# One more pair of MLP chunks in seven products, twelve operand splits on GpSimd, and holds in the order model

## The chip, the core and the metric

The kernel runs on one core of a Trainium2 chip. The core has five engines that run side by side and wait for each other by semaphores: TensorE (PE in the profile; PEld is its weight load), VectorE (DVE), ScalarE (ACT), GpSimd (POOL) and SyncE (SP), which here only issues transfers. On-chip data lies in SBUF, 128 partitions wide; TensorE writes to PSUM, eight banks of 128 x 512 float32. Inputs and outputs lie in DRAM. The metric is the time of one execution on the device, in microseconds; a kernel's time is the median of several runs.

## The reference

Everything is float32. `x` has 2048 tokens of 512 features. Two branches read the layer-normed tokens, and the result is the sum of both and of `x`:

```python
xn = _layernorm(x)                                    # over the 512 features
q, k, v = split(xn @ wqkv)                            # 32 heads of 16
pq, pk = phi(q), phi(k)                               # phi(t) = (t + 1 if t > 0 else exp(t)) + 1e-6
kv, z  = einsum("bhsd,bhse->bhde", pk, v), pk.sum over tokens
o      = einsum(pq, kv) / (einsum(pq, z) + 1e-6)      # linear attention
h      = relu(xn @ w1 + b1) ** 2                      # 1376 hidden columns
return x + o @ wo + (h @ w2 + b2)
```

## The kernel before

**Float32 from two parts.** TensorE multiplies in a format with fewer bits. So every operand is split in two: ScalarE copies it into the short format (the high part), and a second engine subtracts that from the original (the low part). A product then takes three passes: high with high, high with low, low with high. `split(h, l, src, eh, el)` does the two steps, `el` naming the engine of the subtraction; `ops_of` (line 522) splits a weight operand and stores it to DRAM for later use; `parts_of` (line 948) splits an activation.

**Stages.** The 2048 tokens are 16 tiles of 128, or four blocks of 512.
1. The start, to about 105 us: for each tile the layer norm (`bn_stats`, `bn_aggr`, then the small `y` operations of `normalise`, which make the root of the variance, and the tile `xp`), the tile turned (on TensorE for the first eight, by moves `xg` on the sync queue and VectorE transposes for the rest), the projection on k (`ps <- wk, xs`), phi, and the sum `acc <- pk, tok` that becomes kv. GpSimd makes the low part of `tok` here.
2. A round `n = 0` for token blocks 3 and 2, to about 257 us, and a round `n = 1` for blocks 1 and 0. Each goes over seven pairs of 128 columns, `k = 0` to 6: two pairs of q (`NQ = 2`) and five of the hidden columns of the MLP (`NP = 5`); a last, narrower chunk `z` is apart.

**Seven products instead of eight.** Two blocks of tokens against two halves of the features and two chunks of columns is a 2x2 by 2x2 product. The first layer (`"1"`) makes it with seven products, with sums of weight quarters as operands (`make_1`, i = 0, 1: plain, 2 to 5: sums, 6: plain). The second layer (`"2"`), from the pair's four results `h[k, 0..3]` to the output, has two forms. In the plain one each of the four results is split and multiplied with both halves of its w2 rows, eight calls of `second` (line 923), six 128x512 matmuls each (two chunks of 128 output columns, three passes). In the seven-product one VectorE first makes four sums of the results (`combinations`, line 1356), seven activations are split, and seven calls follow, one of each of seven kinds, with w2 operands of plain quarters (`make_m`, `make_m3`) and of sums of quarters (`make_t`). In round 1 all pairs use seven. In round 0 only the two q pairs do (their "w2 rows" are a matrix that the kernel made of kv and wo); the five MLP pairs are plain: their first two results right in the loop (`add_product`), the last two behind the seven products (`plain`). The operands of sums for round 1 (`t` for the MLP pairs) are made in a spare moment at the end of round 0 and the begin of round 1, from rows read a second time (`raw_t`, `made`).

**Buffers.** Weight operands pass through eight SBUF buffers `D0` to `D7` in the order of a list, `needed_in`; in round 0 an entry makes the operand and stores it, otherwise it loads it back. `fetch_raws` reads raw weights into up to four buffers in the order of `raw_jobs`.

**The order of the work.** All operations are recorded first (so every row of the profile has the line of the recorder, 301). `Program.order` then plays the program 150 times with a cost model: TensorE keeps the recorded order, and each other engine takes, of its tasks that are ready, the one with the earliest due time (line 277). After each play the due times of what TensorE waited for are pressed earlier, and the best play's order is emitted. In the model a task with `lock` (lines 155 and 158) waits for the one before it with `lock`: the two-input operations of VectorE with both inputs in SBUF, if they have more than 64 elements, and GpSimd's subtractions.

Of the kernel before, what the change touches and what calls it, by code (L numbers as in the profile page):

```python
# [15 lines left out]
LAST = 3  # L16
REORDER = True
# [57 lines left out]
class Program:  # L75
# [163 lines left out]
    def play(self):  # L239
# [18 lines left out]
        while done < len(ts):  # L258
# [54 lines left out]
def kernel(  # L313
# [20 lines left out]
    TB = 4  # L334
# [110 lines left out]
    NK = NQ + NP  # L445
    wd1 = [dram.tile([4, P, 2, 512], F32, name=f"wd1_{k}") for k in range(NK)]
# [160 lines left out]
    def make_m3(o):  # L607
        for e, k in enumerate((NP, NP + 1)):
            parts_in(o[:, e:e + 1], raw_of[f"2_{k}"][0][:, 1:, 256:])
            spill("2", k, 3, o[:, e:e + 1])  # L610
        m_done(NP, NP + 1)

    def make_t(k, e):

        def make(o):
            raw = f"{'t' if k < NP else '2'}_{k}"
# [9 lines left out]
            if k >= NP:  # L626
                m_done(k)
            elif e:
                raw_done(raw)
# [206 lines left out]
    def needed_in(n):  # L836
# [6 lines left out]
        for p in range(NK + 1):  # L843
# [5 lines left out]
            if f >= 0 and n == 0:  # L849
                both_of("2", f, 0, make_2(f, 0))  # L850
# [6 lines left out]
            if p < NK:  # L857
                both_of("1", p, 4, make_1(p, 4) if direct else None)
                if f >= 0 and n == 0:
# [4 lines left out]
        if n == 0:  # L864
            for k in (NP, NP + 1):
                o.append(([("2", k, 0), ("2", k, 2)], make_m(k)))
                if k == NP:
                    both_of("2", NP - 1, 2, make_2(NP - 1, 1))
            for k in (NP, NP + 1):
                for e in range(2):  # L870
                    both_of("2", k, 4 + 2 * e, make_t(k, e))
            both_of("z", 0, 2, make_z(1))
            o.append(([("2", NP, 3), ("2", NP + 1, 3)], make_m3))
            for f in range(NP):
# [283 lines left out]
    for k in range(NP):  # L1158
        if k + 1 < NP:
            raw_jobs.append(raw_1(NQ + k + 1))  # L1160
        raw_jobs.append(raw_2(k))
    raw_jobs += [raw_2(NP), raw_2(NP + 1), RAW_Z[1]]
# [137 lines left out]
    for n in range(2):  # L1300
# [5 lines left out]
        def slots_of(k):  # L1306
# [8 lines left out]
            else:  # L1315
                t = four(f"rf{k}", f"r{(1, 4, 5)[(k - NQ) // 2]}")
                for e in range(2):
                    slots[k + e] = [None, None, t[:, 2 * e], t[:, 2 * e + 1]]
            return slots[k]
# [4 lines left out]
        def finish(k, i, src):  # L1324
# [9 lines left out]
            else:  # L1334
# [5 lines left out]
                if i < 2:  # L1340
# [15 lines left out]
        def combinations(k):  # L1356

            a, b, c, d = (h[k, i] for i in range(4))
            o = s2[k // 4][:, k % 4] if n else w512(f"s2_{k}", "p", 6)
# [16 lines left out]
        for p in range(NK + 1):  # L1376
# [20 lines left out]
            if f_before:  # L1397
# [4 lines left out]
                add_product(p - 1, 0)  # L1402
# [20 lines left out]
            if f_before:  # L1423
# [36 lines left out]
        if n == 0:  # L1460
            jobs = []
            b = [bank(f"late{k}", loop_tag) for k in range(TB)]
            X, V, Z, Y = b[1:3], [b[3], b[0]], acc[:2], acc[2:]

            def product_job(ps, k, i, first=False, last=False):

                def source():
                    if i not in (0, 2) and k not in h:
                        run(*combinations(k))
                    return h[k, i // 2] if i in (0, 2) else h[k][i]  # L1470

                jobs.append((source, lambda s: second(ps, ("2", NP + k, i), s, first, last)))

            for k in range(NQ):
                product_job(X, k, 0, k == 0)
# [4 lines left out]
            for k in range(NQ):  # L1480
                product_job(V, k, 4, k == 0)
            at_end(lambda: o.update(m5=copies("m5", V)))
            for k in range(NQ):
                product_job(X, k, 5)
# [3 lines left out]
            for k in range(NQ):  # L1488
                product_job(X, k, 6)
            at_end(lambda: o.update(u3=copies("u3", X)))  # L1490
            for k in range(NQ):
                product_job(Y, k, 3, False, k == NQ - 1)
            at_end(lambda: (add_to(o["m5"], Y), turned_to(t1, 2, o["m5"]), store(res[t1], t1, 1)))
            for k in range(NQ):
                product_job(X, k, 7)
# [14 lines left out]
            for k in range(NQ, NK):  # L1510
# [11 lines left out]
            def step(e):  # L1522
# [3 lines left out]
                if e > 3:  # L1526
                    if not made_t and sorted(raw_free) == ["rp0", "rp1", "x0", "x1"]:
# [3 lines left out]
                    if len(raw_free) < 4:  # L1531
                        for u in range(2 * (len(made_t) < NP)):
# [4 lines left out]
            assert len(made_t) >= NP, made_t  # L1537
# [86 lines left out]
```

## Time and profile before

| | |
|---|---|
| median of 3 runs | 409.05 us (408.73 to 409.63) |
| the profiled execution's own time | 408.82 us |
| its span in the profile | 407.1 us |
| TensorE busy | 399.6 us, 1793 matmuls |
| VectorE busy | 353.2 us, 600 instructions |
| ScalarE busy | 269.4 us |
| GpSimd busy | 28.0 us |
| transfers | 95.68 MB, mean 235 GB/s |

A row of a group names engine, operation, what is written and read, shape and count, then busy time and mean of one in ns, then the idle time before these instructions and what ended it. A row of a timeline has the start and the length in us, and in brackets the idle time ahead. Names have no buffer numbers: `ops` are weight operands, `s` split activations, `c` and `rf` the results of MLP pairs in round 0, `rr` other results, `ps` and `acc` the PSUM banks. A busy TensorE is not TensorE at its peak, since its matmuls overlap.

### The profile page before, as it was taken

The numbers are of one execution on the slowest core, as the hardware profiler recorded it, in microseconds if no ns is written. First come the engines' busy times: TensorE is split into PE (matmuls) and PEld (weight loads), VectorE is DVE, ScalarE is ACT, GpSimd is POOL, SyncE is SP. The second block draws the span as 40 slices with busy tenths as digits, with TensorE's granted clock in tenths as the row PEclk, the third lists the DMA queues.
The fourth block names the chain that finished last, engine by engine and source line by source line (L and its number), as shares of the span: only waits on it lengthen the run. The fifth ranks groups of instructions, "written<-read, shape, count | busy, mean of one in ns | idle before, by whom it ended". The sixth has DMA issues, their size and how long they took to land.

```text
span 407.1 us, 5594 instructions
## 1 busy us (share of the span) xinstructions
PE 399.6 (98%) x1793; PEld 330.4 (81%) x1793; DVE 353.2 (87%) x600; ACT 269.4 (66%) x461; POOL 28.0 (7%) x50
## 2 busy tenths in 40 slices
PE   8999999999999999999999999999999999999994
PEld 7787888788888888888888888888888888888883
DVE  5899898799878898999889989899989989786784
ACT  5785665675858897889886343366888777545440
POOL 2232322220000000000000000000000000000001
PEclk9999999999999999999999999999999999999999
DMA  7871455933997679667359998999767789979424
GB/s 230 292 194 43 104 155 125 280 100 151 327 323 287 233 280 306 248 241 260 155 194 361 258 339 275 370 298 330 280 223 271 263 219 258 256 277 281 157 54 103
DMA packets 78674, 95.68 MB, mean 235 GB/s; under 512 B 39186, under 2 KB 50450, under 8 KB 78388
## 3 DMA queue, kind: packets, MB, share of 16 engines
q1 hardware_dynamic: 76404, 94.53, 73.4%
q10 hardware_dynamic: 2144, 0.52, 0.6%
q0 software_dynamic: 96, 0.26, 0.3%
q8 instruction: 14, 0.23, 0.2%
q14 instruction: 16, 0.13, 0.1%
HBM read 57.81 MB, written 35.39 MB: 229 GB/s over the span
## 4 chain that ended last, share of the span: by engine, by line
PE 95%; DVE 2%; DMA 1%; ACT 1%; issue 0%
PE ps L301 52%; PE acc L301 42%; DMA x<-in_A_x_dram 1%; DVE y L301 1%; DVE xp L301 0%; DVE res L301 0%; DVE o L301 0%; DVE st L301 0%; ACT k L301 0%; DVE pk L301 0%; DVE xs0l L301 0%; ACT t L301 0%; ACT xs0h L301 0%; DVE mv L301 0%
## 5 line engine op out<-in xcount | busy, mean ns | idle before, releaser
L301 PE MATMUL ps<-s,ops 128*128 128x512 f32 x405 | 94.9, 389 | 0.0
L301 PEld LDWEIGHTS ps<-s,ops 128*128 128x128 f32 x405 | 76.0, 188 | 15.8
L301 PE MATMUL acc<-s,ops 128*128 128x512 f32 (+1 forms) x270 | 62.2, 382 | 0.0
L301 PEld LDWEIGHTS acc<-s,ops 128*128 128x128 f32 x270 | 49.6, 188 | 9.9
L301 ACT ACTIVATE s<-rr 128x512 fp32r<-128x512 f32 x54 | 33.8, 631 | 20.9 <-DVE s L301 12.0
L301 PE MATMUL acc<-pk,tok 128*128 128x512 f32 x192 | 47.2, 394 | 0.0
L301 DVE TENSOR_TENSOR s<-rr,s 128x512 fp32r<-128x512 f32 x54 | 36.8, 688 | 11.8 <-ACT s L301 10.6
L301 PEld LDWEIGHTS acc<-pk,tok 128*128 128x128 f32 x192 | 35.4, 188 | 8.3 <-DVE pk L301 0.6
L301 PE MATMUL ps<-T,ops 128*128 128x512 f32 x168 | 41.4, 390 | 0.0
L301 PE MATMUL acc<-T,ops 128*128 128x512 f32 x168 | 41.2, 389 | 0.0
L301 PEld LDWEIGHTS acc<-T,ops 128*128 128x128 f32 x168 | 31.5, 188 | 6.6
L301 PEld LDWEIGHTS ps<-T,ops 128*128 128x128 f32 x168 | 31.5, 188 | 6.5
L301 POOL TENSOR_TENSOR tok<-xp,tok 128x512 fp32r<-128x512 f32 x16 | 21.5, 1347 | 43.8 <-ACT tok L301 43.8
L301 PE MATMUL ps<-xs0h,ops 128*128 128x512 f32 x72 | 23.7, 389 | 0.0
L301 ACT ACTIVATE rr<-acc 128x512 f32<-128x512 f32 x23 | 13.6, 589 | 11.5 <-PE acc L301 11.1
L301 DVE TENSOR_TENSOR ops<-raw,ops 128x512 fp32r<-128x512 f32 (+1 forms) x28 | 18.7, 676 | 1.6 <-ACT ops L301 1.6
L301 ACT ACTIVATE ops<-raw 128x512 fp32r<-128x512 f32 (+1 forms) x28 | 15.8, 576 | 5.2 <-PE acc L301 1.8
L301 PE MATMUL acc<-xs0h,ops 128*128 128x512 f32 x56 | 18.4, 389 | 0.0
L301 DVE TENSOR_TENSOR rr<-acc,rr 128x512 f32<-128x512 f32 x21 | 14.4, 687 | 2.9 <-PE acc L301 1.6
L301 POOL DMA_DIRECT2D out_dram<-res x2 | 1.5, 729 | 215.5 <-DVE res L301 213.0
L301 ACT ACTIVATE k<-ps 128x512 f32<-128x512 f32 x16 | 9.5, 593 | 10.1 <-PE ps L301 9.9
L301 PEld LDWEIGHTS ps<-xs0h,ops 128*128 128x128 f32 x72 | 13.5, 188 | 2.8
(158 smaller groups left out, 772.1 us busy)
## 6 DMA issues: line engine op xcount, KB each, us to landing
wd<-ops SPq DMA_DIRECT2D x35, 512.0 KB, 4.8
ops<-wd SPq DMA_DIRECT2D x31, 512.0 KB, 5.5
ops<-wd SPq DMA_DIRECT2D x56, 256.0 KB, 4.1
wd<-made SPq DMA_DIRECT2D x10, 512.0 KB, 5.9
res<-in_A_x_dram SPq DMA_DIRECT2D x32, 128.0 KB, 5.6
wd<-ops SPq DMA_DIRECT2D x13, 256.0 KB, 3.7
out_dram<-res SPq DMA_DIRECT2D x24, 128.0 KB, 4.7
x<-in_A_x_dram SPq DMA_DIRECT2D x5, 512.0 KB, 5.9
```

The source lines that it names most:

```text
L301: getattr(getattr(self.nc, t.engine), t.name)(*map(real, t.args), **{k: real(a) for k, a in t.kw.items()})
```

## The change

Three parts. (1) `SEVEN = 1`: in round 0 the last MLP pair (k = 6, w2 rows 4) joins the two q pairs in the seven products. Its four results are squared at once and kept; the call of `second` for it in the loop and its two plain jobs are gone; the place of the former is taken by the first two products of the first q pair. Its operands for w2 are made by `make_m`, `make_t`, `make_m3` from one buffer of raw rows, and the `t` operands of this pair are stored then, not made later; its rows are fetched last. Each pair's sums are now made in two steps, with the products of kind 4 and of kind 5. (2) In `make_1` the low part of operands i = 2 and 4, for k = 1 to 6, goes to GpSimd: twelve splits, two of them for a q pair, each of a tile with two operands. (3) In the order model the condition on the size is dropped, and where the chosen task has a lock that is held, one that can start is taken before it.

```diff
+SEVEN = 1
...
-            t.lock = t.name in ("tensor_tensor", "scalar_tensor_tensor") and n > 64 and not any(map(in_psum, ins))
+            t.lock = t.name in ("tensor_tensor", "scalar_tensor_tensor") and not any(map(in_psum, ins))
...
                 t = min((t for t in waiting[e] if t.ready <= when + 0.1), key=lambda t: (t.due, t.index))
+                if t.lock and locked > when + 0.1:
+                    t = min((t for t in waiting[e] if max(t.ready, locked * t.lock) <= when + 0.1), key=lambda t: (t.due, t.index), default=t)
...
+    late_pairs = tuple(range(NK - SEVEN, NK))
+    seven_rows = (*range(NP, NP + NQ), *range(NP - SEVEN, NP))
...
-            ops_of(o, "1", k, i, src)
+            ops_of(o, "1", k, i, src, "pool" if k and i in (2, 4) else "dve")
...
-            for k in (NP, NP + 1):
+            for k in seven_rows:
                 o.append(([("2", k, 0), ("2", k, 2)], make_m(k)))
-                if k == NP:
-                    both_of("2", NP - 1, 2, make_2(NP - 1, 1))
-            for k in (NP, NP + 1):
+            for k in seven_rows:
                 for e in range(2):
                     both_of("2", k, 4 + 2 * e, make_t(k, e))
...
-            for f in range(NP):
+            for f in range(NP - SEVEN):
                 for i in (0, 2):
                     both_of("2", f, i)
...
-    raw_jobs += [raw_2(NP), raw_2(NP + 1), RAW_Z[1]]
+    raw_jobs += [raw_2(NP), raw_2(NP + 1), RAW_Z[1], *map(raw_2, seven_rows[NQ:])]
...
-                add_product(p - 1, 0)
+                if n or p - 1 not in late_pairs:
+                    add_product(p - 1, 0)
+                else:
+                    b = [bank(f"late{k}", loop_tag) for k in range(TB)]
+                    X, V, Z, Y = b[1:3], [b[3], b[0]], acc[:2], acc[2:]
+                    for i, ps in ((0, X), (2, Z)):
+                        second(ps, ("2", NP, i), parts_of("s", h[0, i // 2]), i == 0)
...
+            pairs = (*range(NQ), *late_pairs)
+            todo = {}
...
+            def phase(ps, i, first=False, last=False):
+                for k in pairs:
+                    product_job(ps, k, i, first and k == 0, last and k == pairs[-1])
+
+            for k in pairs[1:]:
+                product_job(X, k, 0)
                 product_job(Z, k, 2)
-                if k == 0:
-                    jobs.append((None, lambda s: add_product(NK - 1, 1)))
...
-            for k in range(NQ):
-                product_job(V, k, 4, k == 0)
+            phase(V, 4, True)
...
-            for k in range(NQ, NK):
+            for k in range(NQ, NK - SEVEN):
                 for i in range(2):
                     plain(k, i)
...
-                        raw_jobs.extend(raw_2(k, "t") for k in range(NP))
+                        raw_jobs.extend(raw_2(k, "t") for k in range(NP - SEVEN))
```

More of the change, by code (lines that the diff above doesn't have):

```diff
@@ L605, in make_m, with make_m3 @@
         return make
-    def make_m3(o):
-        for e, k in enumerate((NP, NP + 1)):
+    def make_m3(o, *ks):
+        for e, k in enumerate(ks):
             parts_in(o[:, e:e + 1], raw_of[f"2_{k}"][0][:, 1:, 256:])
             spill("2", k, 3, o[:, e:e + 1])
-        m_done(NP, NP + 1)
+        m_done(*ks)
     def make_t(k, e):
         def make(o):
-            raw = f"{'t' if k < NP else '2'}_{k}"
+            raw = f"{'2' if k in seven_rows else 't'}_{k}"
             (b11, b12), (b21, b22) = ((t[:, 0], t[:, 1]) for t in (by_halves(raw_of[raw][0][:, e]) for e in range(2)))
@@ L625, in make @@
             ops_of(o, "2", k, 4 + 2 * e, by_chunks(src))
-            if k >= NP:
+            if k in seven_rows:
                 m_done(k)
@@ L848, in needed_in @@
                 both_of("1", p, 2, make_1(p, 2) if direct else None)
-            if f >= 0 and n == 0:
+            if f >= 0 and n == 0 and f not in seven_rows:
                 both_of("2", f, 0, make_2(f, 0))
@@ L858, in needed_in @@
                 both_of("1", p, 4, make_1(p, 4) if direct else None)
-                if f >= 0 and n == 0:
+                if f >= 0 and n == 0 and f not in seven_rows:
                     both_of("2", f, 2, make_2(f, 1))
@@ L1339, in finish @@
                 h[k, i] = o
-                if i < 2:
+                if n == 0 and k in late_pairs:
+                    square(o)
+                elif i < 2:
                     square(o)
@@ L1422 @@
             finish(p, 2, R[2])
-            if f_before:
+            if f_before and (n or p - 1 not in late_pairs):
                 add_product(p - 1, 1)
@@ L1461 @@
             jobs = []
-            b = [bank(f"late{k}", loop_tag) for k in range(TB)]
-            X, V, Z, Y = b[1:3], [b[3], b[0]], acc[:2], acc[2:]
+            pairs = (*range(NQ), *late_pairs)
+            todo = {}
             def product_job(ps, k, i, first=False, last=False):
                 def source():
[L1468 to L1472, printed above, removed]
-            for k in range(NQ):
-                product_job(X, k, 0, k == 0)
+                    if i in (0, 2):
+                        return h[k, i // 2]
+                    if i == 4:
+                        todo[k] = combinations(k)
+                    if i in (4, 5):
+                        todo[k].pop(0)()
+                    return h[k][i]
+                jobs.append((source, lambda s: second(ps, ("2", row_of(k), i), s, first, last)))
+            def phase(ps, i, first=False, last=False):
[3 more added lines that the diff above has]
+                product_job(X, k, 0)
                 product_job(Z, k, 2)
-                if k == 0:
-                    jobs.append((None, lambda s: add_product(NK - 1, 1)))
             at_end(lambda: o.update(m1=copies("m1", X)))
-            for k in range(NQ):
-                product_job(V, k, 4, k == 0)
+            phase(V, 4, True)
             at_end(lambda: o.update(m5=copies("m5", V)))
-            for k in range(NQ):
-                product_job(X, k, 5)
+            phase(X, 5)
             at_end(lambda: add_to(o["m5"], X))
@@ L1526, in step @@
                 if e > 3:
[L1527 removed]
+                    if not made_t and not raw_of and not raw_jobs:
+                        assert sorted(raw_free) == ["rp0", "rp1", "x0", "x1"]
                         raw_free[:] = ["x0", "x1"]
[L1529 removed]
+                        raw_jobs.extend(raw_2(k, "t") for k in range(NP - SEVEN))
                         fetch_raws()
[L1531 to L1532 removed]
+                    if made_t or "t_0" in raw_of:
+                        for u in range(2 * (len(made_t) < NP - SEVEN)):
                             make_t(len(made_t), u)(work.tile([P, 2, 512], F32R, name="made", tag=f"rp{u}"))
```

25 lines of the change are left out of this document (14 added, 11 removed).

## The prediction

> **What bounds the kernel now.** I read the page first (engines, clock, chain), then the chain of waits in order of time, then the timeline of each engine where the chain leaves TensorE, then groups of lines by window.
>
> ```profile
> span 407.1 us, 5594 instructions
> PE 399.6 (98%) x1793; PEld 330.4 (81%) x1793; DVE 353.2 (87%) x600; ACT 269.4 (66%) x461; POOL 28.0 (7%) x50
> PEclk9999999999999999999999999999999999999999
> PE 95%; DVE 2%; DMA 1%; ACT 1%; issue 0%
> ```
> ```profile
> 0.81 2.71 DMA x<-in_A_x_dram
> ...
> 75.20 2.72 PE ps L301 x12
> 77.93 3.01 PE acc L301 x12
> 80.94 2.72 PE ps L301 x12
> ...
> 128.09 14.96 PE ps L301 x66
> ...
> 224.65 32.64 PE ps L301 x144
> ...
> 390.61 8.85 PE ps L301 x39
> ```
>
> The page gives TensorE 95% of the chain at a full clock all along. The chain shows how full it is: 32.64 / 144 and 14.96 / 66 are both 0.227 us for a 128x512 matmul, the same as 2.72 / 12. So from 81 us to the last matmul TensorE runs without a gap, VectorE's 87% notwithstanding, and there a matmul less is worth 0.227 us. Only ahead of 81 us do I find lost time: 3.01 where twelve matmuls take 2.72 (0.29 us), and two more places:
>
> ```profile
> 31.07 1.07 PE L301 MATMUL ps<-wkh,xs0l 128*128 128x512 f32 x4
> 32.59 0.65 PE L301 MATMUL ps<-ident,xp 128*128 128x128 f32 x4 [0.46 <-DVE xp L301]
> ...
> 37.66 1.07 PE L301 MATMUL ps<-wkh,xs0l 128*128 128x512 f32 x4
> 38.65 0.66 PE L301 MATMUL ps<-ident,xp 128*128 128x128 f32 x4
> ```
>
> Four matmuls from 31.07 occupy 0.91 us, so the transposes could start at 31.98 and start at 32.59: 0.61 us lost. In the same way 37.66 + 0.91 = 38.57 against 38.65: 0.08. What is late at 32.59 is the normalised tile xp, and VectorE and GpSimd tell why:
>
> ```profile
> 30.32 1.25 DVE L301 SCALAR_TENSOR_TENSOR y<-mv,y 128x2 f32<-128x2 f32 x1
> 31.60 0.36 DVE L301 SCALAR_TENSOR_TENSOR y<-y 128x2 f32<-128x2 f32 x2
> 31.99 1.92 DVE L301 TENSOR_SCALAR xp<-x,mv,y 128x512 f32<-128x512 f32 x4
> ...
> 30.02 1.53 POOL L301 TENSOR_TENSOR tok<-xp,tok 128x512 fp32r<-128x512 f32 x1 [3.21 <-ACT tok L301]
> ...
> 25.55 0.63 ACT L301 ACTIVATE ops<-raw_z 128x512 fp32r<-128x512 f32 x1 [1.07 <-DMA raw_z<-in_B_w_dram]
> 26.25 0.60 ACT L301 ACTIVATE k<-ps 128x512 f32<-128x512 f32 x1
> ```
>
> A two-element operation on y takes 1.25 us, where two of its kind take 0.36 together: it stands behind GpSimd's split of tok (30.02 to 31.55). Before that, ScalarE stood 1.07 us for the load of raw_z, with k behind it. At 75 us VectorE stands for another load, and the 0.29 follows:
>
> ```profile
> 75.23 0.69 DVE L301 TENSOR_TENSOR wv<-wv,raw_v 128x512 f32<-128x512 f32 x1 [2.40 <-DMA raw_v<-in_A_wqkv_dram]
> ```
>
> **The change, part by part.**
>
> *The pair in seven products.* In the first round a plain pair costs eight calls of `second`, the seven-product form seven; a call is six matmuls. Order of the built programs: TensorE issues six 128x512 matmuls fewer, nothing else on it is added. They leave the gapless stretch: 6 x 0.227 = **-1.36 us**. The pair's last two chunks no longer feed TensorE directly behind their relu; their place there is taken by the first attention pair, long finished, so no wait is added.
>
> What it puts on the others lies mostly at 204 to 257 us, where the seven products and the plain pairs run; the first row is of that window, the other two are of the spare operands made for round 1, of the window 245 to 320 us:
>
> ```profile
> 204.00:257.00 53.00, 53.00 (x236) 43.88 (x235) 48.46 (x73) 25.62 (x42) 0.00 (x0) 1.00 0.93 289
> ...
> L301 DVE TENSOR_TENSOR made<-t,made 128x512 fp32r<-128x512 f32 x10 | 6.8, 683 | 0.0
> L301 DVE TENSOR_TENSOR t<-raw_t,t 128x256 f32<-128x256 f32 x10 | 4.2, 422 | 0.2
> ```
>
> VectorE gains three splits and four sums, seven times about 0.69 us: +4.8. The pair's transposed sums and their splits (four operations of 0.42, two of 0.68, 3.0 us) move in from behind 257 us. 48.5 + 7.8 = 56.3 us against the 51.6 that TensorE then takes: by busy time VectorE would be the new bound. But the records of neighbours overlap:
>
> ```profile
> 163.91 0.69 DVE L301 SCALAR_TENSOR_TENSOR rr<-rr,dr 128x512 f32<-128x512 f32 x1
> 164.52 0.69 DVE L301 TENSOR_TENSOR s<-c,s 128x512 fp32r<-128x512 f32 x1
> 165.12 0.68 DVE L301 TENSOR_TENSOR rf<-ps,rf 128x512 f32<-128x512 f32 x1
> 165.72 0.68 DVE L301 TENSOR_TENSOR ops<-s,ops 128x512 fp32r<-128x512 f32 x1
> ```
>
> They start 0.60 us apart and are recorded as 0.69, so the real need is nearer 56.3 x 0.60 / 0.69 = 49.0 us of 51.6, and part of the work there (the split x and the sums for round 1) may also wait until TensorE is in round 1. I take 0 for this part; the other end is that VectorE lags by one operation, 0.7 us, at three of the phases, +2.1. ScalarE gains three copies of 0.63 in a stretch where it is busy 25.6 of 53: 0, by that row.
>
> The pair's w2 rows now stay in their raw buffer until all of the pair's operands are made. In the issue order of the sync queue five transfers of 512 KB are gone (a second load of the raw rows, two stores of spare operands, two reloads) and three stores of 256 KB are added: 1.8 MB less, in a stretch whose transfers are busy at 0.93. The only transfer in the chain is the first load of x, at 0.81 us; I take 0, with a late operand load at +0.5 on the far side.
>
> *GpSimd's twelve splits.* These are what moves, who runs them, and what it costs VectorE when it meets one:
>
> ```profile
> L301 DVE TENSOR_TENSOR ops<-s,ops 128x512 fp32r<-128x512 f32 x12 | 8.2, 680 | 0.0
> L301 DVE TENSOR_TENSOR s<-c,s 128x512 fp32r<-128x512 f32 x9 | 6.1, 674 | 1.0 <-ACT s L301 1.0
> ...
> 65.45 1.78 DVE L301 TENSOR_TENSOR ops<-raw,ops 128x512 fp32r<-128x512 f32 x1
> 67.16 0.68 DVE L301 TENSOR_TENSOR ops<-raw_z,ops 128x512 fp32r<-128x512 f32 x1
> ...
> 65.35 1.34 POOL L301 TENSOR_TENSOR tok<-xp,tok 128x512 fp32r<-128x512 f32 x1 [3.09 <-ACT tok L301]
> ```
>
> The first two rows are of the window 97 to 197 us. VectorE loses 8.2 us; GpSimd, idle there, gains 12 x 1.34 = 16 us. The operand is ready 0.65 us later for the product and for its store to DRAM; the eight buffers ahead of TensorE hide that. A VectorE operation with both inputs in SBUF that is issued under GpSimd's split takes 1.78 instead of 0.68: up to 1.10 lost per split, 13.2 us for twelve, more than the 8.2 saved. The Trainium skill (SBUF — State Buffer, Who interferes with whom) says so too: a VectorE instruction with two SBUF inputs and a GpSimd instruction that reads SBUF exclude each other for the whole instruction. By that rule the edit alone is a loss for VectorE of up to 5.0 us of its time; the trace agrees (1.78 against 0.68). Were all of it on TensorE's path, the sum would be 5.0 higher, 411.7. What counts for the time is whether a held operation is one that TensorE awaits:
>
> ```profile
> 163.51 0.63 ACT L301 ACTIVATE s<-c 128x512 fp32r<-128x512 f32 x1
> 164.05 0.58 ACT L301 ACTIVATE rf<-ps 128x512 f32<-128x512 f32 x1
> 164.53 0.62 ACT L301 ACTIVATE ops<-s 128x512 fp32r<-128x512 f32 x1
> ...
> 164.64 1.75 PE L301 MATMUL acc<-s,ops 128*128 128x512 f32 x7
> ```
>
> This is the tightest place of a step. The split s<-c ends on VectorE at 165.21; TensorE reads it with its fifth matmul, at 164.64 + 4 x 0.227 = 165.55: 0.34 us to spare. A hold of 1.10 in front of it costs 0.76. In the new order ScalarE's copy for GpSimd stands behind its copy for s<-c in these steps, so GpSimd can begin some 0.5 us after VectorE may (the ScalarE rows start 0.54 and 0.48 apart), and behind s<-c come an operation from PSUM, a reciprocal and a transpose, with one SBUF input each. I take 0, far end 9 x 0.76 = +6.8, near end 0: VectorE freed of 8.2 us cannot speed a gapless TensorE.
>
> *The order model.* It now counts a hold for operations of any size, and passes over a held task for a free one. It changes the order of VectorE, ScalarE and the sync queue from about 23 us on; TensorE's order and the order behind the last matmul stay. The second y group (the one of 30.32) now stands directly behind pk and one bn_stats instead of behind two bn_stats, k, xs0l and pk, and ahead of the tok split; its roots on ScalarE, still behind raw_z, stand behind xs0h alone instead of behind k, k, xs0h, t and pk. That is some four VectorE operations of 0.6 us and the hold earlier, against a lateness of 0.61: I count **-0.61**, and **-0.08** for the next tile, whose y is likewise earlier. The subtraction from wv that waited 2.40 us now stands behind k and pk of the next tile, and the load of raw_v ahead of a store on the sync queue: **-0.29**. Each can come back elsewhere among so many short dependences; far end of the three together 0, or +0.5 when the new order has a wait of its own.
>
> *Sum.* The profiled execution took 408.82 us. 408.82 - 1.36 - 0.61 - 0.08 - 0.29 = 406.48. It lies 0.23 under the median of 409.05, so the forecast for the median is **406.7 us**. The end is untouched: from 399.46 on the old order stands.
>
> **The rivals.**
>
> *Only the six matmuls count.* The start's waits are only moved. For it: so many small dependences, and the loads of raw_z and raw_v land when they land. Against it: the y group is earlier by more than its lateness. 409.05 - 1.36 = 407.7.
>
> *VectorE becomes the bound between 204 and 257 us.* For it: 56.3 of 51.6 by busy time, 49.0 by starts. Against it: what can wait there. Three lags of 0.7 give back 2.1 of what was won: 406.7 + 2.1 = 408.8, no measurable change.
>
> *GpSimd's hold falls on the awaited splits.* Slower: each held s<-c costs 0.76; from four of the nine on (3.0 us) the gain of 2.3 is gone. Five give 406.7 + 3.8 = 410.5, all nine 413.5. For it: the rows at 65.45 show the hold in full; GpSimd starts when its input is there, not when the order model thinks. Against it: the order of ScalarE's copies.
>
> **How the numbers follow.** The forecast (all of the sum) has 0.55, only the six matmuls 0.22, VectorE as the bound 0.13, the hold 0.10. A measurement of this kernel tells about 0.2%, 0.8 us, from no change. Faster by more: the first two and a little of the third, 0.79; within: 0.12; slower: 0.09. The range 406.2 to 408.6 reaches from 0.5 under the forecast (the first 30 us may give some more) over 407.7 to the edge of the third case. The forecast alone would be 406.3 to 407.2.
>
> **What would show it.** Right: 1787 matmuls; from 81 us on groups of 0.227 us a matmul; no 0.46 before ident,xp at 32 us; twelve rows ops<-s on GpSimd near 1.3 us; VectorE nearly full from 204 to 257 us, and TensorE without a gap there. Wrong: TensorE behind DVE s or POOL ops in the list of waits; a y row of over 1 us again ahead of an xp that TensorE awaits; a piece of the chain between 110 and 200 us above 0.227 us a matmul.

## The result, and the profile after

The changed kernel takes 406.94 us (median of six runs, 406.76 to 407.24), the kernel before took 409.35 us beside it (median of six, 408.73 to 410.06). The ratio is 0.9941, with a 95% interval of 0.9929 to 0.9954: 2.4 us faster, where 406.7 was forecast. The execution that was profiled took 407.24 us, the longest of its six, over a span of 405.5 us; that of before had 408.82. So the two profiled executions are only 1.58 us apart; the rest of the 2.4 lies between executions.

The page of the changed kernel, its first rows and the shares of its chain:

```profile
span 405.5 us, 5588 instructions
PE 397.9 (98%) x1787; PEld 329.3 (81%) x1787; DVE 353.6 (87%) x595; ACT 270.7 (67%) x464; POOL 46.3 (11%) x62
DMA packets 78258, 93.85 MB, mean 231 GB/s; under 512 B 39154, under 2 KB 50418, under 8 KB 77972
PE 96%; DVE 2%; DMA 1%; issue 0%
```

The six matmuls are gone (1793 to 1787), and so are the 1.8 MB. GpSimd has its twelve splits, 18.3 us more busy than before, but VectorE is as busy as it was (353.2 before), although it has five instructions fewer. TensorE still makes the chain, and in its two longest pieces on `ps` it runs at the same pace as before:

```profile
127.02 14.96 PE ps L304 x66
...
163.74 2.88 PE acc L304 x12
...
226.64 28.56 PE ps L304 x126
```

28.56 / 126 = 0.227 us a matmul, also where the third pair of seven products runs. But two short pieces stand out: twelve matmuls from 163.74 take 2.88, not 2.72 us, and twelve from 178.85 take 2.91. The start, in the timelines of VectorE, GpSimd and TensorE:

```profile
27.78 0.16 DVE L304 SCALAR_TENSOR_TENSOR y<-mv,y 128x2 f32<-128x2 f32 x1 [0.52 <-ACT y L304]
27.98 0.36 DVE L304 SCALAR_TENSOR_TENSOR y<-y 128x2 f32<-128x2 f32 x2
28.37 0.55 DVE L304 TENSOR_SCALAR xp<-x,mv,y 128x512 f32<-128x512 f32 x1
...
30.75 1.30 POOL L304 TENSOR_TENSOR tok<-xp,tok 128x512 fp32r<-128x512 f32 x1 [3.89 <-DVE st L304]
...
31.10 1.07 PE L304 MATMUL ps<-wkh,xs0l 128*128 128x512 f32 x4
32.01 0.60 PE L304 MATMUL ps<-ident,xp 128*128 128x128 f32 x4
```

The y operation that lasted 1.25 us now lasts 0.16 and ends 2.8 us before GpSimd's split of tok begins, and the transposes follow the matmuls ahead of them without a gap (31.10 + 0.91 = 32.01).

For all kernels below I use one account, worked out from the starts of the matmuls in the trace, from the 41st (at 10.2 to 10.7 us) to the last: every distance over 0.26 us counts as a wait with what it has above 0.227, and the rest of the stretch is TensorE without waits. Before: 390.76 us, of which 1.80 are waits. After: 388.70, of which 1.17 are waits. Without waits that is 388.96 and 387.52, or 1.44 less; the waits give 0.63. Short ones that every kernel has, 0.09 to 0.11 each and most of them where TensorE turns to another accumulator, are 0.86 us of each sum, which is all that the kernel with the fewest has left (e12). The account is of one profiled execution each, and it ends at the last matmul. Behind that the changed kernel lost some of its lead: from VectorE's last operation to the end of the span, with the last stores under way, 4.5 us passed before (402.57 to 407.1) and 5.0 after (400.53 to 405.5). Over all fourteen profiled executions the time from the start of the last matmul to the end of the span lies between 5.6 and 6.6 us; why it varies isn't known.

### The profile page after: what moved, and what is told of

Same layout as the page of the kernel before. It is cut to its first block, busy times and chain, and to the rows that moved or that the text cites. A ratio compares the mean times of both kernels' runs of the same rounds, so it can differ in the third digit from the quotient of the medians.

```text
span 405.5 us, 5588 instructions
## 1 busy us (share of the span) xinstructions
PE 397.9 (98%) x1787; PEld 329.3 (81%) x1787; DVE 353.6 (87%) x595; ACT 270.7 (67%) x464; POOL 46.3 (11%) x62
## 4 chain that ended last, share of the span: by engine, by line
PE 96%; DVE 2%; DMA 1%; issue 0%
PE ps L304 53%; PE acc L304 43%; DMA x<-in_A_x_dram 1%; DVE res L304 0%; DVE o L304 0%; DVE st L304 0%; DVE xp L304 0%; DVE y L304 0%; DVE mv L304 0%
## 5 line engine op out<-in xcount | busy, mean ns | idle before, releaser
L304 PE MATMUL ps<-s,ops 128*128 128x512 f32 x411 | 96.4, 389 | 0.0
L304 PEld LDWEIGHTS ps<-s,ops 128*128 128x128 f32 x411 | 77.1, 188 | 16.0
L304 PE MATMUL acc<-s,ops 128*128 128x512 f32 (+1 forms) x258 | 59.8, 383 | 0.0
L304 PEld LDWEIGHTS acc<-s,ops 128*128 128x128 f32 x258 | 47.2, 188 | 9.9 <-ACT s L304 0.5
L304 ACT ACTIVATE s<-rr 128x512 fp32r<-128x512 f32 x56 | 34.9, 630 | 21.1 <-DVE s L304 11.0
L304 DVE TENSOR_TENSOR s<-rr,s 128x512 fp32r<-128x512 f32 x56 | 38.1, 686 | 9.4 <-ACT s L304 8.3
L304 POOL TENSOR_TENSOR tok<-xp,tok 128x512 fp32r<-128x512 f32 x16 | 23.1, 1442 | 43.7 <-ACT tok L304 26.9
L304 POOL TENSOR_TENSOR ops<-s,ops 128x512 fp32r<-128x512 f32 x12 | 16.7, 1396 | 75.5 <-ACT ops L304 58.1
L304 DVE TENSOR_TENSOR ops<-raw,ops 128x512 fp32r<-128x512 f32 (+1 forms) x28 | 17.4, 630 | 0.7 <-ACT ops L304 0.5
```

The lines of the kernel that those rows point to most:

```text
L304: getattr(getattr(self.nc, t.engine), t.name)(*map(real, t.args), **{k: real(a) for k, a in t.kw.items()})
```

## The experiments

My theory was the sum of the prediction: six matmuls, plus start's waits that the two lines of the order model remove, with the GpSimd splits worth nothing. The rivals: that any edit makes the planner draw another order, and the waits come and go with it; that the splits are needed, since VectorE has more to do with a third pair in seven products; that their holds cost time.

| kernel | pair k = 6 | splits | model | median, us | ratio to before | waits | without waits |
|---|---|---|---|---|---|---|---|
| before | eight | VectorE | old | 408.9 to 409.4 | 1 | 1.80 | 388.96 |
| e1 | eight | VectorE | new | 408.42 | 0.9984 (0.9975 to 0.9993) | 1.67 | 388.84 |
| e3 | eight | GpSimd | old | 408.33 | 0.9984 (0.9975 to 0.9993) | 1.52 | 388.78 |
| e6 | eight | GpSimd, order of before | old | 408.84 | 0.9996 (0.9987 to 1.0005) | 2.07 | 388.89 |
| e8 | eight | VectorE, redrawn | old | 408.36 | 0.9985 (0.9976 to 0.9994) | 1.45 | 388.84 |
| e9 | eight | VectorE, order of before, repaired | old | 407.99 | 0.9969 (0.9956 to 0.9981) | 1.33 | 388.79 |
| e2 | seven | VectorE | old | 408.44 | 0.9993 (0.9984 to 1.0002) | 1.92 | 387.63 |
| e4 | seven | VectorE | new | 409.01 | 0.9999 (0.9990 to 1.0008) | 3.12 | 387.47 |
| e11 | seven | GpSimd | old | 408.07 | 0.9970 (0.9960 to 0.9980) | 3.16 | 387.49 |
| after | seven | GpSimd | new | 406.94 | 0.9941 (0.9929 to 0.9954) | 1.17 | 387.52 |
| e5 | seven | VectorE, order of after | new | 407.12 | 0.9952 (0.9940 to 0.9965) | 1.25 | 387.55 |
| e7 | seven | GpSimd, redrawn | new | 406.37 | 0.9936 (0.9924 to 0.9949) | 1.08 | 387.51 |
| e10 | seven | GpSimd, order of after, two swaps | new | 406.70 | 0.9934 (0.9921 to 0.9946) | 0.98 | 387.37 |
| e12 | seven | GpSimd, redrawn again | new | 406.60 | 0.9933 (0.9921 to 0.9946) | 0.86 | 387.37 |

### One part alone, and all but the splits

The order model alone, on the kernel before:

```diff
-            t.lock = ... and n > 64 and not any(map(in_psum, ins))
+            t.lock = ... and not any(map(in_psum, ins))
...
+                if t.lock and locked > when + 0.1:
+                    t = min((t for t in waiting[e] if max(t.ready, locked * t.lock) <= when + 0.1), ...)
```

> The kernel before with the two lines of the order model alone: 1793 matmuls, no split on GpSimd added, eight calls for the pair k = 6. My theory (the lines of the model remove the start's waits): the waits of 0.61 us ahead of ident,xp at 32.6 us, 0.08 at 38.7 and 0.29 at 78 us go and nothing takes their place: 0.98 us less, a ratio of 0.9976. Rival (re-planning): any edit makes the planner draw another order, and the start's waits come and go by chance: then this kernel has waits of its own before 81 us, of a sum that may lie on either side of 0.98 us, ratio 0.999 to 1.001. Rival (six matmuls only): ratio 1.000.

0.9984, 0.6 us. The waits at 32.6 and 78 us are gone, but a longer one stands at 26.49, and it is of the very kind that the new lines describe. Its rows, in the timelines of VectorE, GpSimd and TensorE:

```profile
24.90 0.57 DVE L303 SCALAR_TENSOR_TENSOR y<-mv,y 128x3 f32<-128x3 f32 x1
25.89 0.55 DVE L303 TENSOR_SCALAR xp<-x,mv,y 128x512 f32<-128x512 f32 x1
...
24.15 1.29 POOL L303 TENSOR_TENSOR tok<-xp,tok 128x512 fp32r<-128x512 f32 x1 [0.89 <-ACT tok L303]
...
26.49 0.66 PE L303 MATMUL ps<-ident,xp 128*128 128x128 f32 x4 [0.66 <-DVE xp L303]
```

The tile xp is late by 0.82 us, and only part of that is the hold of y (0.57 instead of 0.16): the group simply stands late in this order.

The seven products alone (the diff of the change without the lines above and without the splits):

> The kernel before with the seven products for the pair k = 6 alone: no GpSimd splits, old model. My theory: six matmuls of 0.227 us less, 1.36 us, a ratio of 0.9967, with the start's waits of 0.98 us still there. Rival (VectorE becomes the bound between 204 and 257 us): three or more lags of 0.7 us of TensorE behind VectorE there, 2.1 us back, a ratio near 1.002. Rival (re-planning): the start's waits differ from those of before although the model is the same, and the ratio lies off 0.9967 by that difference.

0.9993, most of the six matmuls' gain lost. Without waits TensorE needs 387.63, as the changed kernel, but the waits are not where either theory put them. The start has none at 32 or 78 us, although the model is the old one, and from 204 to 257 us there are only 0.2 us of them. The largest stands at 150, here with VectorE's row ahead of it:

```profile
148.54 0.69 DVE L302 TENSOR_TENSOR rf<-ps,rf 128x512 f32<-128x512 f32 x1
149.15 0.68 DVE L302 TENSOR_TENSOR s<-c,s 128x512 fp32r<-128x512 f32 x1
...
149.88 0.72 PE L302 MATMUL acc<-s,ops 128*128 128x512 f32 x2 [0.39 <-DVE s L302]
```

Its s<-c stands behind a transpose and rf<-ps, where before had it ahead of rf (164.52 in the prediction's rows): 0.56 us of TensorE for a place in a queue, as these rows read.

The splits alone:

```diff
-            ops_of(o, "1", k, i, src)
+            ops_of(o, "1", k, i, src, "pool" if k and i in (2, 4) else "dve")
```

> The kernel before with the twelve splits on GpSimd alone: old model, eight calls for the pair k = 6. My theory: VectorE is freed of 8 us and TensorE does not move: ratio 1.000, start's waits as before. Rival (the hold): the old order does not know where GpSimd stands, and each s<-c split that falls under a GpSimd split costs TensorE 0.76 us: for four of nine 3.0 us, a ratio of 1.007. Rival (copies): ScalarE's copies for GpSimd stand ahead of its copies for s<-c and cost TensorE 0.1 to 0.23 us each, a few tenths in all.

0.9984. No loss by holds, and again a start without its waits, with the old model; small ones stand at 220 us instead.

The changed kernel with the splits back on VectorE:

```diff
-            ops_of(o, "1", k, i, src, "pool" if k and i in (2, 4) else "dve")
+            ops_of(o, "1", k, i, src)
```

> The changed kernel with the twelve splits back on VectorE: seven products for k = 6 and the new model stay. My theory (the splits are worth nothing to TensorE): as the changed kernel, a ratio of 0.994; the three small waits of TensorE behind ScalarE's copies at 163.9, 179.0 and 277.1 us, 0.1 us each at the matmul, may go, for 0.996 to 0.993. Rival (relief): with seven products VectorE needs the 8 us that GpSimd takes off it; without them TensorE waits for VectorE's s or c rows, 0.7 us or more in all, a ratio of 0.996 or above.

0.9999: the whole gain is gone. That looks like the relief. But of its 3.12 us of waits, 0.88 stand at 32.8 us, ahead of ident,xp, where none of the twelve splits is concerned. VectorE and GpSimd show what is late there:

```profile
29.55 1.96 DVE L304 TENSOR_SCALAR xp<-x,mv,y 128x512 f32<-128x512 f32 x2
...
32.20 0.55 DVE L304 TENSOR_SCALAR xp<-x,mv,y 128x512 f32<-128x512 f32 x1
...
29.76 1.46 POOL L304 TENSOR_TENSOR tok<-xp,tok 128x512 fp32r<-128x512 f32 x1 [2.99 <-ACT tok L304]
```

Two xp in a row take 1.96 us here and 1.00 us in the changed kernel (at 33.31): the second begins under GpSimd's split of tok. This is a hold of 0.96 us, on an operation with one input of 512 elements, and neither order model has it, since both lock two-input operations alone. VectorE has no gap from there to the xp at 32.20 that TensorE awaits, so by these rows this hold is the whole wait; no run here removes it to test that.

The largest of the other waits is one for a single copy of ScalarE, which itself waited for VectorE's t. Timelines of ScalarE and TensorE:

```profile
210.96 0.67 ACT L304 ACTIVATE ops<-t 128x512 fp32r<-128x512 f32 x1 [1.03 <-DVE t L304]
...
211.69 1.22 PE L304 MATMUL ps<-s,ops 128*128 128x512 f32 x3 [0.42 <-ACT ops L304]
```

Four kernels, four different sets of waits. So a part can't be priced by building it in or out: the planner draws the whole order anew each time.

### The splits with the order held still

In the next two the plan is made as in the changed kernel (or as before), and only when the tasks are emitted is the engine of the twelve subtractions exchanged. Every queue keeps its order; nothing else differs.

```diff
-            getattr(getattr(self.nc, t.engine), t.name)(
+            getattr(getattr(self.nc, "vector" if t.moved else t.engine), t.name)(
...
         split(o[:, 0], o[:, 1], src, "act", el)
+        nc.tasks[-1].moved = el == "pool"
```

> The changed kernel with its planned order kept in every queue, only the twelve subtractions carried out by VectorE at the places of that order instead of GpSimd. Theory (relief: with the pair in seven products VectorE needs the twelve operations taken off it): twelve times 0.60 us come back on VectorE where s<-c had 0.36 to 0.45 us to spare, so TensorE waits behind VectorE's s or c rows between 97 and 257 us, 1.3 us in all as in the two kernels with seven products and without the splits (gaps of 1.26 and 1.39 us there), a time of 408.2 or more. Rival (the planner's draw: the lags of those two kernels are of their own orders): no gap, 406.9, a ratio of 0.994 to before.

407.12 us against 406.94 (ratios 0.9952 and 0.9941, with intervals that overlap), and the waits are 1.25 against 1.17: the runs can't tell the two apart, with or without GpSimd. In this order the relief is not needed. The page of this kernel, a window of it, and the same window with the one behind it in the changed kernel (length, then busy time of PE, PEld, DVE, ACT and POOL, clock, share of the DMA engines, GB/s):

```profile
PE 397.8 (98%) x1787; PEld 329.1 (81%) x1787; DVE 356.1 (88%) x607; ACT 270.5 (67%) x464; POOL 29.5 (7%) x50
```

```profile
97.00:197.00 100.00, 100.00 (x457) 82.80 (x456) 90.74 (x159) 83.61 (x139) 0.52 (x1) 1.00 0.77 268
```

```profile
97.00:197.00 100.00, 100.00 (x457) 82.94 (x456) 88.42 (x147) 83.72 (x139) 17.27 (x13) 1.00 0.77 267
204.00:257.00 53.00, 53.00 (x235) 43.88 (x235) 48.82 (x73) 25.35 (x43) 0.00 (x0) 1.00 0.93 272
```

Twelve operations more cost VectorE 2.5 us of busy time, not the 8.2 of their rows (12 x 0.68). About 1.0 of the other 5.7 is the overlap of neighbouring records (0.60 from start to start instead of 0.68); the remaining 4.7 I put down to the holds in the changed kernel, an estimate. The other way round, the order of before with GpSimd as the engine:

> The kernel before with its planned order kept in every queue, only the twelve subtractions carried out by GpSimd. Theory: TensorE had no wait behind VectorE after 81 us, so relief is worth nothing here, ratio 1.000. Rival (the hold): the order was made without GpSimd in it, so its splits start when ScalarE's copy is there and hold VectorE's two-input operations by up to 1.1 us each; every s<-c among them costs TensorE 0.76 us, four of nine a ratio of 1.007. In the trace: gaps of TensorE at 110 to 197 us behind s<-c rows of over 1 us.

Ratio 0.9996, the same. Here a hold does fall on an s<-c. The timelines of VectorE, GpSimd and TensorE, and then the row of the page:

```profile
138.27 1.52 DVE L302 TENSOR_TENSOR s<-c,s 128x512 fp32r<-128x512 f32 x1
...
149.20 0.68 DVE L302 TENSOR_TENSOR s<-c,s 128x512 fp32r<-128x512 f32 x1
150.51 1.28 DVE L302 TENSOR_TENSOR ops<-raw,ops 128x256 fp32r<-128x256 f32 x1
...
137.94 1.29 POOL L302 TENSOR_TENSOR ops<-s,ops 128x512 fp32r<-128x512 f32 x1 [10.08 <-ACT ops L302]
...
150.21 1.30 POOL L302 TENSOR_TENSOR ops<-s,ops 128x512 fp32r<-128x512 f32 x1 [6.30 <-ACT ops L302]
...
142.83 2.88 PE L302 MATMUL acc<-s,ops 128*128 128x512 f32 x12
```

```profile
PE 398.5 (98%) x1793; PEld 329.7 (81%) x1793; DVE 352.0 (86%) x588; ACT 269.3 (66%) x461; POOL 44.7 (11%) x62
```

1.52 us at 138.27, but TensorE multiplies by no s before 142.83, and has no gap there. At the tight places, as at 149.20, GpSimd's split begins 1.0 us after s<-c and holds a split of an operand instead, which TensorE doesn't see. VectorE is 1.2 us less busy than before (352.0 against 353.2) for 8.2 us of work taken off it. With the same 1.0 for overlap some 6.0 came back as holds, and TensorE saw none of it.

### The planner's draw

One number of the model is moved, which changes no instruction, only the order:

```diff
-    DVE = {..., "tensor_tensor": (0.157, 1.0), "scalar_tensor_tensor": (0.157, 1.0), ...
+    DVE = {..., "tensor_tensor": (0.160, 1.0), "scalar_tensor_tensor": (0.160, 1.0), ...
```

> The changed kernel with one number of the order model moved a little (0.157 to 0.160 us for VectorE's two-input operations), so that the planner settles on another order of the same work. Theory (the gain is that of the parts): the same to 0.3 us, 406.6 to 407.2. Rival (the draw): the waits at the start (0.6 to 1.1 us ahead of ident,xp) or small waits at 100 to 260 us come back, and the time moves by 0.5 to 2 us with nothing changed in the work.

> The kernel before with the same number of the order model moved (0.157 to 0.160 us). Theory (the start's waits are what the old model leaves behind): they stay, ratio 1.000. Rival (the draw): the waits of 0.61, 0.08 and 0.29 us go or others come, ratio 0.997 to 1.003.

The kernel before moves to 408.36 us, by 0.54 us against the runs beside it (ratio 0.9985, an interval that ends below 1), with nothing changed in the work; that is against the theory. The changed kernel comes out at 406.37, just below the theory's range, and no wait came back in it; but its ratio, 0.9936, can't be told from 0.9941, and the runs of before beside it were faster too (408.90 against 409.35 us). The redrawn kernel of before has no wait at 32 us either, with the old model, and instead 0.23 us at 56 and 0.37 at 78 us. The other direction (0.154), later:

> The changed kernel with the number of the order model for VectorE's two-input operations moved the other way (0.157 to 0.154 us). Theory (draw): six matmuls less and waits of its own, 406.2 to 408.8. If the parts gave the gain rather than the draw: 406.4 to 407.2, without a wait of TensorE over 0.15 us behind 10 us.

406.60 us; the list of waits of TensorE has one entry left, the first one of the program:

```profile
PE ps L304 <- DVE odds L304: 1.1, 1, 1.1
```

The changed kernel with the model's lines taken back:

```diff
-            t.lock = ... and not any(map(in_psum, ins))
+            t.lock = ... and n > 64 and not any(map(in_psum, ins))
...
-                if t.lock and locked > when + 0.1:
-                    t = min((t for t in waiting[e] if max(t.ready, locked * t.lock) <= when + 0.1), ...)
```

> The changed kernel with the order model of before (both lines taken back): seven products and GpSimd's splits stay. Theory (draw: the lines of the model do not decide whether the start's waits are there): 1.36 us less by six matmuls, and start's waits of any size between 0 and 1.0, so 406.4 to 407.7, ratio 0.994 to 0.997; lags behind VectorE at 97 to 257 us of up to 1.4 us are drawn likewise. Rival (the lines remove the start's waits): the waits ahead of ident,xp near 32 us and of acc at 78 us are back with about 0.98 us in sum, and the time is 407.6 to 408.0.

408.07 us, just above the ranges of both readings. The start's waits aren't back: none at 32 or 78 us. The waits are at 53.10, at 211 and at 243.12. TensorE's timeline, with ScalarE's row ahead of the second:

```profile
53.10 0.50 PE L302 MATMUL ps<-wkh,xs1h 128*128 128x512 f32 x1 [0.68 <-ACT xs1h L302]
...
243.12 0.70 PE L302 MATMUL ps<-s,ops 128*128 128x512 f32 x2 [0.69 <-ACT s L302]
...
242.47 0.63 ACT L302 ACTIVATE s<-hz 128x512 fp32r<-128x512 f32 x1 [2.09 <-PE ps L302]
```

GpSimd splits nothing near either place, so they aren't holds that the old model missed.

### Two places repaired by hand

The kernel before, its order kept but for the y group and one subtraction from wv:

```diff
+        for n, i in enumerate((236, 237, 240, 241, 242, 243)):
+            ts[i].start = 31.60 + 0.01 * n
+        ts[544].start = ts[545].start - 0.01
         return sorted(ts, key=lambda t: (t.start, t.index))
```

> The kernel before with its planned order, in which two things alone are moved by hand: the second y group of the start (two ScalarE and three VectorE operations of two elements, and the tile xp behind them) to directly behind xs0l, ahead of bn_stats and pk and so ahead of GpSimd's split of tok; and the first subtraction from wv to directly ahead of the second, so that VectorE does not stand 2.4 us for raw_v with k behind it. Theory (these two places are the 0.61 and the 0.29 us): both gaps of TensorE at 32.6 and 78 us go, 0.90 us, a ratio of 0.9978; the y row lasts 0.15 instead of 1.25 us. Rival (the wait is only moved: pk, now behind xp, or the next tile is late instead): a new gap of 0.3 us or more between 32 and 45 us or at 75 to 90 us, ratio 0.999 or above.

The first place behaves as told. VectorE and TensorE at the start:

```profile
29.03 0.15 DVE L304 SCALAR_TENSOR_TENSOR y<-mv,y 128x2 f32<-128x2 f32 x1
...
29.61 0.55 DVE L304 TENSOR_SCALAR xp<-x,mv,y 128x512 f32<-128x512 f32 x1
...
30.68 1.18 DVE L304 SCALAR_TENSOR_TENSOR pk<-k,pk 128x512 fp32r<-128x512 f32 x1
...
31.89 0.60 PE L304 MATMUL ps<-ident,xp 128*128 128x128 f32 x4
```

The hold now falls on pk (1.18 us), which has time, and the 0.62 of TensorE is gone. The second place does not: VectorE no longer stands for raw_v, and yet TensorE loses 0.24 and 0.08 us at 77.2 to 77.6, where it lost 0.17 and 0.08. ScalarE shows why:

```profile
75.36 0.63 ACT L304 ACTIVATE ops<-raw 128x512 fp32r<-128x512 f32 x1 [1.10 <-DMA raw<-in_A_wqkv_dram]
76.15 0.42 ACT L304 ACTIVATE ops<-raw 128x256 fp32r<-128x256 f32 x1 [0.16 <-DMA raw<-in_A_wqkv_dram]
76.48 0.62 ACT L304 ACTIVATE pk<-k 128x512 fp32r<-128x512 f32 x1
```

pk stands behind two copies that wait for another load. Two waits ended at the same time; removing one leaves the other. The median falls by 1.32 us, while the waits of the profiled executions fall only by 0.47; the rest lies between these executions and their medians (408.82 against 409.31 for before, 408.22 against 407.99 here), and where it arises in the unprofiled runs isn't known.

The changed kernel, its order kept, with ScalarE's copy for s<-c ahead of rf<-ps at two places:

```diff
+        for i, j in ((1345, 1360), (1453, 1469)):
+            ts[i].start = ts[j].start - 0.01
         return sorted(ts, key=lambda t: (t.start, t.index))
```

> The changed kernel with its planned order, in which ScalarE's copy for s<-c changes places with its copy rf<-ps ahead of it at two places (162.4 and 177.5 us). Theory (TensorE's gaps there are a wait for ScalarE's copy, which stands behind a copy that nobody awaits): both gaps of 0.11 us go, the one at 277.1 us stays; the time falls by 0.2 us. Rival (the gap is the first use of a new accumulator or of a new operand, whoever made it): gaps of 335 to 341 ns start to start stay at both places, the time stays. Rival (rf is then late: VectorE's rf<-ps and the phi behind it): a gap behind it within 3 us.

In the changed kernel ScalarE and TensorE's weight load show this:

```profile
162.41 0.60 ACT L304 ACTIVATE rf<-ps 128x512 f32<-128x512 f32 x1
162.91 0.62 ACT L304 ACTIVATE s<-c 128x512 fp32r<-128x512 f32 x1
...
163.58 2.38 PEld L304 LDWEIGHTS acc<-s,ops 128*128 128x128 f32 x11 [0.27 <-ACT s L304]
```

and with the swap this:

```profile
162.42 0.63 ACT L306 ACTIVATE s<-c 128x512 fp32r<-128x512 f32 x1
162.96 0.58 ACT L306 ACTIVATE rf<-ps 128x512 f32<-128x512 f32 x1
...
163.33 2.71 PEld L306 LDWEIGHTS acc<-s,ops 128*128 128x128 f32 x12
```

Both gaps are gone, the one at 277 stays, and nothing behind is late. The waits fall from 1.17 to 0.98. The time, 406.70 us, can't be told from 406.94: the ratios are 0.9934 and 0.9941, with intervals that overlap. Of all kernels the redrawn ones are the fastest (406.37 and 406.60 us); their intervals overlap with the changed kernel's.

## Why the prediction came out right, step by step

**The six matmuls, -1.36: right.** Over six kernels with eight calls the stretch without waits is 388.78 to 388.96 us, mean 388.85; over eight with seven it is 387.37 to 387.63, mean 387.49. The difference of the means is 1.36 = 6 x 0.227. Single executions of one kind differ by up to 0.26, which is why before and after alone give 1.44.

**VectorE between 204 and 257 us, 0: right in the result, wrong in the size.** I worked out 56.3 us of busy time; the changed kernel has 48.82, as many instructions as before (73). What can wait does wait: the sums for round 1 (t<-raw_t and made) take 4.8 us of VectorE in this window before and 0.8 after. Other work moves back behind them, and from 300 to 399 us VectorE is 3.5 us busier than before. The sign that I named, VectorE nearly full from 204 to 257 us, is not borne out: it is hardly fuller than before (48.46). The transfers, which I also took as 0, are busy at 0.93 there in both kernels, and TensorE's list of waits names no transfer. These are the later windows of before and, behind it, of the changed kernel:

```profile
300.00:399.00 99.00, 99.00 (x438) 81.98 (x437) 82.43 (x130) 60.45 (x100) 0.80 (x1) 1.00 0.78 229
```

```profile
300.00:399.00 99.00, 99.00 (x445) 82.25 (x444) 85.93 (x135) 59.02 (x97) 0.93 (x2) 1.00 0.78 216
```

The rival of VectorE as the bound falls with it for this order. Even with the twelve splits on VectorE (e5) TensorE doesn't wait for it. Other orders of the same seven products do lose time there: e4 has 1.06 us of waits at 210 to 213 us, behind VectorE's t, and e11 has 1.35 at 211 and 243 us.

**The GpSimd splits, 0: right, for the reason given.** With the order held still the exchange of the engine moved nothing that the runs resolve, in either kernel (407.12 against 406.94; ratio 0.9996, 0.9987 to 1.0005). The holds stay within the forecast (1.52 for 0.68 us, where I had up to 1.78), they eat some 4.7 to 6.0 of the 8.2 us saved, and they fall where TensorE doesn't look, since ScalarE copies for s<-c first: in the changed kernel none of the eight s<-c rows from 97 to 197 us is held (0.65 to 0.69 us), in e6 one of nine. The Trainium skill (SBUF — State Buffer, Who interferes with whom) has the rule for the holds, and the traces agree with it. The loss of up to 5.0 us of VectorE's time that I worked out by it isn't there: with the order held still VectorE ended 1.2 and 2.5 us less busy.

**The order model, -0.98: right in size, wrong in cause.** In the changed kernel the waits of 0.62, 0.09 and 0.25 us are gone. But the step said that the two lines do it, and the runs don't bear that out: four kernels with the old model (e2, e3, e8, e11) have no wait at 32 us, and two with the new one (e1, e4) have waits of 0.82 and 0.88 ahead of ident,xp. What removed them is the new draw of the order, and that it removed them in full is in part luck. The model's lines are also too narrow. In the fourteen traces every xp that begins under a split of tok lasts 0.63 to 1.59 us, every other one at most 0.55, but xp has no lock in the model; in the changed kernel that costs nothing (1.48 us at 30.85), in e4 it comes to 0.96 of VectorE, ahead of the wait of 0.88. Within the step, 0.61 was the hold of y and its late place (e9 removes it by moving y alone), but the 0.29 was not raw_v alone: ScalarE's pk behind a wait for raw ended just as late.

**A term that I didn't have: three new waits behind ScalarE's copies,** 0.11, 0.11 and 0.09 us at 163.9, 179.0 and 277.1 us. I looked only at whether VectorE's half of s<-c comes in time and priced ScalarE's order as a help; its own half was the later one at the first two. At 277.1 us it is its copy rr<-acc (276.15, 0.58 us long) that TensorE's next use of the accumulator waits for. The sign of being wrong that I had named, a piece of the chain above 0.227 us a matmul between 110 and 200 us, came with these waits (2.88 / 12 = 0.240). 1.36 + 0.98 - 0.31 = 2.03 us is what the steps then give for the stretch from 10 us on, where the trace has 2.06.

**Luck in the number.** The sum was for the profiled execution: 406.48 us. That took 407.24, which is 0.76 more: 0.31 by the three new waits, and about 0.45 at the end behind the last matmul, which I had taken as untouched. The median came within 0.24 us of the forecast because the profiled execution of before lay below its median and the one of the changed kernel lies 0.30 above.

**The rival of the six matmuls alone** (407.7) was worth more than its 0.22: e2, e4 and e11 have seven products and end at 408.1 to 409.0, since their orders hold 1.9 to 3.2 us of waits. All three draws with all three parts ended at 406.4 to 406.9, the three with seven products and one or both of the other parts missing (and an order of their own) did not. That points to the planner finding good orders more easily when it has splits on GpSimd and the holds in its model. Six draws don't settle it; and since e5 keeps the order and needs no GpSimd, the splits would help the planner then, not the chip.

## What to carry to other kernels

Where one engine runs without a gap, count its instructions: over fourteen kernels that term came out at 1.36 us between the means, with a scatter of 0.2 to 0.3 between single executions. Where a planner sets the order, an edit is also a new draw: to price the edit hold the order still and exchange only the edit, and to price the draw move a number that changes no work. When a wait is to be removed, look at every queue that ends there; what ends second-latest there is all that can be gained.

## What was not expected of the hardware

The hold works in both directions: in the changed kernel a GpSimd split that begins under VectorE's rr<-rr,dr lasts 1.80 us, where one that begins beside an operation from PSUM lasts 1.30. Its rows, with VectorE's, in the two timelines:

```profile
118.96 0.69 DVE L304 TENSOR_TENSOR rr<-ps,rr 128x512 f32<-128x512 f32 x1 [0.39 <-ACT ops L304]
...
156.29 0.68 DVE L304 SCALAR_TENSOR_TENSOR rr<-rr,dr 128x512 f32<-128x512 f32 x1
...
156.33 1.80 POOL L304 TENSOR_TENSOR ops<-s,ops 128x512 fp32r<-128x512 f32 x1 [5.84 <-ACT ops L304]
...
118.98 1.30 POOL L304 TENSOR_TENSOR ops<-s,ops 128x512 fp32r<-128x512 f32 x1 [7.84 <-ACT ops L304]
```

I had counted holds on VectorE alone. The Trainium skill says in the section named above that whoever issues first keeps the other waiting; these rows agree.

And an operand that comes late for a weight load costs less than its lateness: the weight load at 163.58 starts 0.23 us later than the one ahead of it would have let it (distance 0.46), while the matmuls lose 0.11. Ahead of it, the load at 163.12 runs 0.23 us before its matmul at 163.35, so part of the lateness falls into that lead.
